# Gate differences at the head of the output products, casts that wait for one of them, and column tiles for two more key products

## The chip, the cores and the metric

The kernel runs on one core of one Trainium2 chip. The metric is device time in microseconds (us) of one execution. Each time below is the median of several executions, with the lowest and highest.

PE is TensorE's matmul stream, PEld its weight loads, DVE is VectorE, ACT ScalarE, POOL GpSimd, SP SyncE (which issues most of the DMAs here).

## The reference

Eight batches, eight heads, 576 tokens, head width 64. Queries are softmaxed over the head width, keys over the tokens; then two products give the attention output, which feeds a feed-forward block with a gate.

```python
kv  = einsum('bhsd,bhse->bhde', softmax(k, tokens), v)
x   = einsum('bhsd,bhde->bhse', softmax(q, width), kv)   # -> (4608, 512)
h   = x @ w_in                                           # (512, 2048)
g   = h * sigmoid(beta * h)
out = g @ w_out                                          # (2048, 512)
```

## The kernel before

The output product is done by a seven-product (Strassen-like) scheme: it needs sums of gate blocks (`g_sum1`, `g_sum2`) and two differences (`g_diff(0)`, the lower one, and `g_diff(1)`, the upper one; both write into the gates GT). A slab is 512 tokens; there are nine, and slabs 0 to 7 are batches 0 to 7 less 64 tokens each, which make up the last slab. `pass 1` is x @ w_in with the gates, `pass2_fast` the seven products. Into slab t's products the kernel mixes the attention work of batch t+1 by a list of (position, function), and calls hooks between products for that of batch t+2. In slabs 1 to 3 those hooks are written out one by one. Instructions of an engine run in the order in which they are added. The code below is abridged; comments stand for what is left out.

```python
def tiled(b):                 # key products as two column tiles of 64
    return b > 3

def attn_late(b):             # attention work of batch b in slab b-1
    ...
    if b < 4:
        s = spread(kv_steps(b, (0, 1)), 97, 101) + spread(kv_steps(b, (2, 3)), 101, 105)
        s += [(105, lambda: g_diff(1))]
        return s + spread(x[0:2], 117, 120)         # x: output steps (kv times QT)
    s = [(96, steps(kv_all, b)), (99, lambda: g_diff(1))]
    return s + spread(x, 107, 123)

def norm_turn(b, hp0):        # sums and 1/sums on DVE, scaling of EQ on POOL, DMA transpose to QT
    norm_main(b, hp0, 2, POOL)
    turn(b, hp0, 2)

def pass2_fast(t, tick, hooks):
    ...
    at(0)
    # product 1 (sums), product 2 (sums)
    # DVE: TS = product 1
    at(1)
    # DVE: TS -= product 2
    at(2)
    # product 3 (sums); DVE: TS -= product 3
    if t > 3:
        g_diff(0)
        g_diff(1)
    at(3)
    # product 4 (lower half, GT), product 5 (GT), product 6 (lower difference), product 7 (upper difference)

def casts(b):                 # POOL casts of the values: six where b is even, four where it is odd
    g = P.writer[("gs2", NG - 1)]                   # not before the last gate sum
    if b % 2 == 0:
        cast_vr(b, after=g)
    for hp in range(NHP):
        cast_v(b, hp, after=g)

if t == 1:
    on(0, exps, 2);  on(0, casts, 2)
    on(2, norm_turn, 2, 0);  on(3, norm_turn, 2, 2)
    on(3, g_diff, 0);  on(3, load, 4)
elif t == 2:
    on(0, exps, 3)
    on(2, norm_turn, 3, 0);  on(3, norm_turn, 3, 2)
    on(3, g_diff, 0);  on(3, load, 5)
    on(4, exp_q, 4);  on(4, casts, 4);  on(6, norm_turn, 4, 0)
```

The first two output steps of a batch below 4 come at positions 117 and 118.5 of the seven products, the last two in the first pass of the next slab, at 1 and 2.5:

```python
todo += [(1, steps(out_step, t, 2, MB, ACTE)), (2.5, steps(out_step, t, 3))]
```

The softmax here doesn't subtract the row's maximum and nothing guards it: scores larger than these inputs give would overflow.

Of the kernel before, what the change touches and what calls it, by code (L numbers as in the profile page):

```python
# [20 lines left out]
NG = NF // 2  # L21
# [134 lines left out]
def bass_efficient_attn_shen__then__act_swish_beta_kernel(  # L156
# [12 lines left out]
    with ExitStack() as es:  # L169
# [52 lines left out]
        P = Program()  # L222
# [156 lines left out]
        def bank(pool=MB):  # L379
            rot[0] += 1  # L380
            return pool[rot[0] % len(pool)]

        def mm(o, l, r_, start, stop, r=(), w=(), bk=0, tr=False):
            if tr:
                add(PE, lambda e: e.transpose(o, l, r_), r=r, w=w, bank=[bk])
            else:
                add(PE, lambda e: e.matmul(o, l, r_, start=start, stop=stop), r=r, w=w, bank=[bk])  # L387
# [22 lines left out]
        def kv_rows(b, hp, j):  # L410
            i = b % 2
            pi = (b // 2) % 2
            if j < 4:
                return (bass.AP(EK[i], hp * 512 + j * 128, [[2048, 128], [1, 128]]),
                        VB[i][:, j, hp, :], [("ek", i, hp)], [("vb", i, hp)], [("vone", i)])
            if b < 2:
                return (bass.AP(EKS[b], hp * 128, [[512, 128], [1, 128]]), VRS[b][:, hp, :],
                        [EKSK[b]], [("vrs", b)],
                        [("vrs0", b), ("vrsone", b, 0), ("vrsone", b, 1)])
            return (bass.AP(EKR[pi], hp * 128, [[512, 128], [1, 128]]),  # L420
                    VR[pi][b % 2][:, hp, :], [("ekr", pi, 0), ("ekr", pi, 1)],
                    [("vr", pi, b % 2)], [("vr0", pi, b % 2), ("vrone", pi, b % 2)])
# [2 lines left out]
            return b if b < 2 else 2 + b % 4  # L425

        def tiled(b):
            return b > 3

        def kvd(b, hp, bk, c):  # L430
            i = b % 2
# [7 lines left out]
        def kv_steps(b, hps, pool=MB):  # L439
            i = b % 2  # L440
            st = {}

            def one(n, hp, j):
                if n == 0 and j == 0:
                    st["b"] = bank(pool)
                bk = st["b"]
                l, r_, ke, kv, ko = kv_rows(b, hp, j)
                if not tiled(b):
                    mm(PS[bk][:, 256 * n:256 * n + VW - 1], l, r_[:, 0:VW - 1], j == 0, j == 4,
                       r=ke + kv, w=[("ps", bk)], bk=bk)  # L450
                for h in range(2) if tiled(b) else ():
                    p = slice(64 * h, 64 * h + 64)
                    add(PE, lambda e, h=h, p=p: e.matmul(  # L453
                        PS[bk][p, 256 * n:256 * n + D + 1], l[:, p], r_[:, HW * h:HW * h + D + 1],
                        start=j == 0, stop=j == 4, tile_position=(0, 64 * h),
                        skip_group_check=True),
                        r=ke + kv, w=[("ps", bk)], bank=[bk])
                if n == len(hps) - 1 and j == 4:
                    c, k_ = hps[0], len(hps)
                    s_ = bass.AP(PS[bk], D, [[512, 128], [256, k_]])  # L460
                    add(DVE, lambda e: e.reciprocal(RC[i][:, c:c + k_], s_),
                        r=[("ps", bk)], w=[("rc", i, h2) for h2 in hps], bank=[bk])
                    for m, h2 in enumerate(hps):
                        kvd(b, h2, bk, 256 * m)
            return [lambda n=n, hp=hp, j=j: one(n, hp, j) for n, hp in enumerate(hps)
                    for j in range(5)]
# [59 lines left out]
        def steps(fn, *a):  # L526
            return lambda: go(fn(*a))
# [12 lines left out]
        def attn_late(b):  # L540
            x = []
            for hp in range(NHP):
                x += out_step(b, hp, MB, ACTE if hp % 2 else DVE)
            if b < 4:
                s = spread(kv_steps(b, (0, 1)), 97, 101) + spread(kv_steps(b, (2, 3)), 101, 105)
                s += [(105, lambda: g_diff(1))]
                return s + spread(x[0:2], 117, 120)
            s = [(96, steps(kv_all, b)), (99, lambda: g_diff(1))]
            return s + spread(x, 107, 123)

        def spread(steps, lo, hi):
            return [(lo + (hi - lo) * k / len(steps), s) for k, s in enumerate(steps)]
# [8 lines left out]
        def go(steps):  # L561
            for s in steps:
                s()
# [154 lines left out]
        def g_diff(fh):  # L718
            f, th = NG * fh, 1 - fh
            add(DVE, lambda e: e.tensor_tensor(gv(f, th, NG), gv(f, th, NG), gv(f, 1 - th, NG),  # L720
                                               ALU.subtract),
                r=gk(f, 0, NG) + gk(f, 1, NG), w=gk(f, th, NG), war=True)
# [20 lines left out]
        def pass2_fast(t, tick, hooks):  # L743
            s, z5, z2 = HB[hrot[0] % 3], OB[0], OB[1]
            z2s = (OB[1], MB[0]) if t == NSLAB - 1 else (z2, z2)

            def prod(bk, lhs, lk, rhs, rk, first, end=False, part=range(NG)):
                two = bk == z2 and z2s[0] != z2s[1]
                for i, u in ([(i, u) for u in range(2) for i in part] if two and end else
                             [(i, u) for i in part for u in range(2)]):  # L750
                    l, r_ = lhs(i, u), rhs(i)
                    st = first and i == 0 and (u == 0 or two)
                    b_ = z2s[u] if two else bk
                    add(PE, lambda e, l=l, r_=r_, st=st, u=u, i=i, b_=b_: e.matmul(  # L754
                        PS[b_][:, 256 * u:256 * u + 256], l, r_, start=st, stop=end and i == NG - 1,
                        skip_group_check=True),
                        r=lk(i) + rk(i), w=[("ps", b_)], bank=[b_])
                    tick(32.0 / 56)

            def gt(f0, th):  # L760
                return (lambda i, u: GT[:, f0 + i, 256 * th + 128 * u:256 * th + 128 * u + 128],
                        lambda i: [("gt", f0 + i, th)])
# [5 lines left out]
            def wo(fh, dh):  # L768
                return (lambda i: WOUT[:, NG * fh + i, 256 * dh:256 * dh + 256],
                        lambda i: [("wout", NG * fh + i, dh)])  # L770
# [39 lines left out]
            def at(n):  # L810
                for f in hooks.get(n, ()):
                    f()

            at(0)
            def prod_s(part):
                prod(s, lambda i, u: GS1[:, i, 128 * u:128 * u + 128], lambda i: [("gs1", i)],
                     *wsum(0), True, True, part)
# [12 lines left out]
            for b_, u0, u1 in halves(z2):  # L830
# [1 line left out]
                add(DVE, lambda e, b_=b_, c=c: e.tensor_tensor(  # L832
                    TS[:, c], TS[:, c], PS[b_][:, c], ALU.subtract),
                    r=["ts", ("ps", b_)], w=["ts"], bank=[b_])
            if t > 3:
                g_diff(0)
                g_diff(1)
            at(3)
            prod(z5, *gt(0, 0), *wo(0, 1), False)
            copy(z5, 0, 1, ACTE)  # L840
            at(4)
# [21 lines left out]
        for t in range(NSLAB):  # L863
# [90 lines left out]
            def on(n, fn, *a):  # L954
                hooks.setdefault(n, []).append(lambda: fn(*a))
# [5 lines left out]
                    exp_kr(b)  # L961

            def casts(b):
                g = P.writer[("gs2", NG - 1)]
                if b % 2 == 0:
                    cast_vr(b, after=g)
                for hp in range(NHP):
                    cast_v(b, hp, after=g)

            if t == 1:  # L970
                on(0, exps, 2)
                on(0, casts, 2)
                on(2, norm_turn, 2, 0)
                on(3, norm_turn, 2, 2)
                on(3, g_diff, 0)
                on(3, load, 4)
            elif t == 2:
                on(0, exps, 3)
                on(2, norm_turn, 3, 0)
                on(3, norm_turn, 3, 2)  # L980
                on(3, g_diff, 0)
                on(3, load, 5)
                on(4, exp_q, 4)
                on(4, casts, 4)
                on(6, norm_turn, 4, 0)
            elif t == 3:
                on(0, exp_k, 4)
                on(0, exp_kr, 4)
                on(0, exp_q, 5)
                on(3, g_diff, 0)  # L990
                on(4, norm_turn, 5, 0)
                on(5, norm_turn, 5, 2)
                on(4, exp_qr)
                on(5, exp_k, 5)
                on(5, norm_turn_rem)
                on(5, casts, 5)
                on(5, load, 6)
                on(7, load_rem, "qrf", qt_h, QRF, 4)
            elif t + 2 < B:
                b = t + 2  # L1000
                on(0, exps, b)
                on(0, casts, b)
                if t == 4:
                    on(0, load, 7)
                on(3, norm_turn, b, 0)
                on(4, norm_turn, b, 2)
# [40 lines left out]
```

## Time and profile before

| | before |
|---|---|
| time, median of 3 | 273.59 us (273.55 to 273.74) |
| profiled span | 271.7 us, clock 1.0 |
| second pass of slab 1 begins | 60.65 us |
| second pass of slab 2 begins | 89.22 us |
| second pass of slab 3 begins | 117.57 us |
| last DVE instruction begins | 268.03 us |

The four marks in the lower rows divide the span into stages: 28.57 us ("slab 1": from its second pass to that of slab 2), 28.35 us ("slab 2", likewise), 150.46 us (the rest). The prediction shows the main lines of this profile. Two more views of it are needed later. First, from the page's table of costly groups: what it was, busy us and mean ns, then idle time of the engine before these instructions and what ended it.

```profile
L754 PE MATMUL PS<-WSUM,GT 128*128 128x256 bf16 x256 | 30.4, 273 | 0.5 <-DMA QT<-EQ 0.4
...
L720 DVE TENSOR_TENSOR GT<-GT 128x2048 bf16<-128x2048 bf16 x16 | 20.1, 1281 | 0.0
```

The products with a difference (PE) wait 0.5 us in the whole run, and 0.4 of it is one wait for the transposed queries. The 16 differences (DVE) take 1.28 us each on average. Second, POOL's timeline in slab 2 (start, length, what; instructions of one kind in a row are put together):

```profile
95.52 4.74 POOL L343 TENSOR_TENSOR EQ<-EQ,QI 128x1024 bf16<-128x1024 bf16 x2 [13.91 <-DVE QI L341]
100.39 2.16 POOL L372 CAST VR<-VRF 64x512 bf16<-64x512 f32 x2
```

The two casts of VR take 2.16 us here. The same two took 1.35 us in slab 1.

### The profile page before, as it was taken

The numbers are of one execution on the slowest core, as the hardware profiler recorded it, in microseconds if no ns is written. First come the engines' busy times: TensorE is split into PE (matmuls) and PEld (weight loads), VectorE is DVE, ScalarE is ACT, GpSimd is POOL, SyncE is SP. The second block draws the span as 40 slices with busy tenths as digits, with TensorE's granted clock in tenths as the row PEclk, the third lists the DMA queues.
The fourth block names the chain that finished last, engine by engine and source line by source line (L and its number), as shares of the span: only waits on it lengthen the run. The fifth ranks groups of instructions, "written<-read, shape, count | busy, mean of one in ns | idle before, by whom it ended". The sixth has DMA issues, their size and how long they took to land.

```text
span 271.7 us, 4811 instructions
## 1 busy us (share of the span) xinstructions
PE 263.8 (97%) x1882; PEld 165.7 (61%) x1905; DVE 194.0 (71%) x416; ACT 181.0 (67%) x284; POOL 64.1 (24%) x80
## 2 busy tenths in 40 slices
PE   8899999999999999999999999999999999999994
PEld 3444444448844885478646865687458745874683
DVE  4964586887867799878786977787687548626762
ACT  4898558789287956897778847893883387018610
POOL 2790010006530089000910870037000100000000
PEclk9999999999999999999999999999999999999999
DMA  7999999989799129930499999203800130012005
GB/s 220 314 201 207 227 321 349 303 227 373 173 337 285 65 53 299 332 95 2 89 282 283 308 345 182 103 20 65 208 0 2 31 142 2 0 69 88 0 5 152
DMA packets 59366, 45.93 MB, mean 169 GB/s; under 512 B 28608, under 2 KB 58320, under 8 KB 58320
## 3 DMA queue, kind: packets, MB, share of 16 engines
q1 hardware_dynamic: 54480, 40.90, 53.4%
q0 software_dynamic: 4240, 4.19, 9.4%
q10 hardware_dynamic: 624, 0.53, 0.6%
q8 instruction: 15, 0.25, 0.4%
q14 instruction: 7, 0.06, 0.1%
HBM read 36.71 MB, written 9.44 MB: 170 GB/s over the span
## 4 chain that ended last, share of the span: by engine, by line
PE 85%; DVE 4%; DMA 4%; POOL 2%; SPq 2%; issue 2%; ACT 1%; POOLq 0%
PE PS L387 51%; PE PS L754 33%; DMA VF<-in_v_dram 2%; DMA QT<-EQ 1%; PE PS L453 1%; POOL VB L358 1%; SPq L275 1%; DVE QS L339 1%; SPq L287 1%; DVE EQ L343 1%; POOL EQ L343 1%; DVE VB L358 1%; ACT GT L654 1%; POOL VR L372 0%; DVE QI L341 0%
## 5 line engine op out<-in xcount | busy, mean ns | idle before, releaser
L387 PE MATMUL PS<-XT,WIN 128*128 128x512 bf16 x562 | 126.2, 379 | 1.1 <-issue 0.3
L654 ACT ACTIVATE GT<-PS,BETA 128x512 bf16<-128x512 f32 x144 | 95.1, 689 | 37.8 <-PE PS L387 37.5
L387 PEld LDWEIGHTS PS<-XT,WIN 128*128 128x128 bf16 x576 | 55.2, 98 | 64.4 <-DVE XT L479 0.6
L677 DVE TENSOR_SCALAR GT<-GT,RB 128x512 bf16<-128x512 bf16 x144 | 52.1, 382 | 36.5 <-ACT GT L654 35.6
L343 POOL TENSOR_TENSOR EQ<-EQ,QI 128x1024 bf16<-128x1024 bf16 (+1 forms) x13 | 25.6, 1967 | 46.9 <-DVE QI L341 46.3
L754 PE MATMUL PS<-WOUT,GT 128*128 128x256 bf16 x256 | 33.0, 273 | 0.1
L754 PE MATMUL PS<-WOUT,GS 128*128 128x256 bf16 x256 | 31.9, 273 | 0.2
L754 PE MATMUL PS<-WSUM,GT 128*128 128x256 bf16 x256 | 30.4, 273 | 0.5 <-DMA QT<-EQ 0.4
L754 PEld LDWEIGHTS PS<-WSUM,GT 128*128 128x128 bf16 x256 | 25.0, 98 | 3.8 <-issue 0.3
L754 PEld LDWEIGHTS PS<-WOUT,GT 128*128 128x128 bf16 x256 | 24.9, 98 | 3.5
L790 ACT COPY O2S<-PS 128x512 f32<-128x512 f32 (+1 forms) x17 | 9.4, 560 | 25.6 <-PE PS L754 24.2
L754 PEld LDWEIGHTS PS<-WOUT,GS 128*128 128x128 bf16 x256 | 24.1, 98 | 3.4
L307 ACT ACTIVATE EQ<-QF 128x512 bf16<-128x512 f32 x32 | 17.9, 620 | 7.3 <-DMA QF<-in_q_dram 7.2
L358 POOL CAST VB<-VF 128x512 bf16<-128x512 f32 x24 | 16.7, 694 | 23.0 <-DVE GS L713 14.1
L713 DVE TENSOR_TENSOR GS<-GT 128x512 bf16<-128x512 bf16 (+2 forms) x32 | 21.9, 685 | 0.0
L339 DVE TENSOR_REDUCE QS<-EQ 128x16 f32<-128x1024 bf16 (+1 forms) x20 | 19.8, 991 | 0.9 <-ACT EQ L307 0.9
L720 DVE TENSOR_TENSOR GT<-GT 128x2048 bf16<-128x2048 bf16 x16 | 20.1, 1281 | 0.0
L307 ACT ACTIVATE EK<-KF 128x512 bf16<-128x512 f32 x32 | 18.1, 620 | 0.1
L479 ACT CAST XT<-PS 128x512 bf16<-128x512 f32 x18 | 10.3, 581 | 10.7 <-PE PS L387 10.7
L802 DVE TENSOR_TENSOR O2S<-TS,PS 128x512 f32<-128x512 f32 (+1 forms) x17 | 10.7, 643 | 9.5 <-PE PS L754 9.5
L754 PE MATMUL PS<-WSUM,GS 128*128 128x256 bf16 x128 | 16.7, 273 | 0.0
L387 PE MATMUL PS<-WOUT,GT 128*128 128x512 bf16 x62 | 15.0, 379 | 0.1
(82 smaller groups left out, 225.5 us busy)
## 6 DMA issues: line engine op xcount, KB each, us to landing
out_dram<-O2S SPq DMA_DIRECT2D x8, 1024.0 KB, 5.4
QF<-in_q_dram SPq DMA_DIRECT2D x6, 1024.0 KB, 5.9
KF<-in_k_dram SPq DMA_DIRECT2D x6, 1024.0 KB, 8.5
VF<-in_v_dram SPq DMA_DIRECT2D x6, 1024.0 KB, 12.2
KF<-in_k_dram SPq DMA_DIRECT2D x8, 256.0 KB, 5.5
VF<-in_v_dram SPq DMA_DIRECT2D x8, 256.0 KB, 5.5
WOUT<-in_moe_w_out_dram POOLq DMA_DIRECT2D x4, 512.0 KB, 16.4
WIN<-in_moe_w_in_dram POOLq DMA_DIRECT2D x3, 512.0 KB, 9.0
```

The lines of the kernel that those rows point to most:

```text
L307: add(ACTE, lambda e, o=o, a=a: e.activation(o, a, ACT.Exp), r=[(name + "f", i, hp)], w=[("e" + name, i, hp)])
L339: add(DVE, lambda e: e.tensor_reduce(s_, a, AX.X, ALU.add), r=ks, w=[("qs", i, hp0)])
L343: add(eng, lambda e: e.tensor_tensor(a, a, vb, ALU.mult), r=ks + [("qi", i, hp0)], w=ks)
L358: add(eng, lambda e: (e.copy if eng == ACTE else e.tensor_copy)(o, a), r=[("vf", i, hp), ("vone", i)], w=[("vb", i, hp)], after=after)
L387: add(PE, lambda e: e.matmul(o, l, r_, start=start, stop=stop), r=r, w=w, bank=[bk])
L479: add(eng, lambda e: (e.copy if eng == ACTE else e.tensor_copy)(XT[i][:, hp, :], PS[bk][:, :]), r=[("ps", bk)], w=[("xt", i, hp)], bank=[bk])
L654: add(ACTE, lambda e: e.activation(GT[:, f, :], PS[bk][:, :], ACT.Silu, scale=BETA[:, f:f + 1]), r=[("ps", bk), "beta"], w=[("gt", f, 0), ...
L677: add(DVE, lambda e: e.tensor_scalar(GT[:, f, :], GT[:, f, :], RB[:, f:f + 1], None, ALU.mult), r=k + ["rb"], w=k)
L713: add(DVE, lambda e: e.tensor_tensor(GS2[:, i:i + n, :], GT[:, i:i + n, :], GT[:, i + NG:i + NG + n, :], ALU.add), r=[k_ for f in (i, i + ...
L720: add(DVE, lambda e: e.tensor_tensor(gv(f, th, NG), gv(f, th, NG), gv(f, 1 - th, NG), ALU.subtract), r=gk(f, 0, NG) + gk(f, 1, NG), w=gk(f ...
L754: add(PE, lambda e, l=l, r_=r_, st=st, u=u, i=i, b_=b_: e.matmul(PS[b_][:, 256 * u:256 * u + 256], l, r_, start=st, stop=end and i == NG - ...
L802: add(DVE, lambda e, b_=b_, u0=u0, u1=u1: e.tensor_tensor(o[:, u0:u1, :], ts[:, u0:u1, :], bank3(b_)[:, u0:u1, :], ALU.add), r=["ts", ("ps ...
```

## The change

The intent, as far as the edit shows it: DVE stands idle before the first sum of the products, so one difference is put there; the other goes where the first sums are done. The differences and POOL's instructions get in each other's way (the prediction shows how), so the casts are made to wait for the upper difference. And the key products of batches 2 and 3 get the cheaper column tiles that batches 4 to 7 have.

```diff
         def tiled(b):
-            return b > 3
+            return b > 1
@@ attn_late
             if b < 4:
-                s = spread(kv_steps(b, (0, 1)), 97, 101) + spread(kv_steps(b, (2, 3)), 101, 105)
-                s += [(105, lambda: g_diff(1))]
+                s = [(101, steps(kv_all, b))]
                 return s + spread(x[0:2], 117, 120)
-            s = [(96, steps(kv_all, b)), (99, lambda: g_diff(1))]
+            s = [(96, steps(kv_all, b))]
@@ pass2_fast
+            g_diff(1)
             at(0)
@@ after the third sum
-            if t > 3:
+            if t > 2:
                 g_diff(0)
-                g_diff(1)
             at(3)
+            if t < 3:
+                g_diff(0)
@@ casts
-                g = P.writer[("gs2", NG - 1)]
+                g = P.writer[("gt", NG, 0)]
@@ hooks of slabs 1, 2 and 3, in each of them
-                on(3, g_diff, 0)
```

More of the change, by code (lines that the diff above doesn't have):

```diff
@@ L980, in bass_efficient_attn_shen__then__act_swish_beta_kernel @@
                 on(3, norm_turn, 3, 2)
-                on(3, g_diff, 0)
                 on(3, load, 5)
@@ L989, in bass_efficient_attn_shen__then__act_swish_beta_kernel @@
                 on(0, exp_q, 5)
-                on(3, g_diff, 0)
                 on(4, norm_turn, 5, 0)
```

## The prediction

> **What bounds the kernel now.** I started from the page's table of engines, then the chain of work that ended last, then the waits of PE and PEld by stretch, then the timelines of the stretches that the change edits.
>
> ```profile
> PE 263.8 (97%) x1882; PEld 165.7 (61%) x1905; DVE 194.0 (71%) x416; ACT 181.0 (67%) x284; POOL 64.1 (24%) x80
> PE 85%; DVE 4%; DMA 4%; POOL 2%; SPq 2%; issue 2%; ACT 1%; POOLq 0%
> ```
>
> The second line is the chain by engine. PE is the bound, at full granted clock, and after the first 50 us it almost never waits. So only two things are worth time: fewer PE cycles, or a change in one of the few PE waits that are left. The program runs nine slabs; each has a first pass (64 matmuls of 512 columns) and a second pass (112 matmuls of 256 columns, seven products). The second passes of slabs 1, 2 and 3 begin near 60.7, 89.4 and 117.6 us, and into those of slabs 1 and 2 the key products of batches 2 and 3 are mixed: these are what the change edits most.
>
> The PE waits left there are all for the transposed queries QT. In slab 1 the chain leaves PE altogether for ten microseconds:
>
> ```profile
> 62.25 0.34 DVE GS L713
> ...
> 62.72 0.61 POOL VR L372
> ...
> 66.22 0.61 POOL VB L358
> ...
> 66.96 1.91 POOL EQ L343
> ...
> 68.88 3.53 DMA QT<-EQ
> 72.41 0.27 issue
> 72.68 0.49 PE PS L754 x3
> ```
>
> Columns are start, length, what. The last sum of the gates (GS, done at 62.59) releases six POOL casts in a row, the scaling of EQ queues behind them on POOL, then comes the DMA transpose, and PE stands still until it lands at 72.41. Here POOL, not PE, sets the time. The timeline of DVE in the same stretch:
>
> ```profile
> 63.90 0.69 DVE L823 COPY TS<-PS 128x512 f32<-128x512 f32 x1 [1.32 <-PE PS L754]
> ...
> 68.51 0.25 DVE L341 RECIPROCAL QI<-QS 128x16 f32<-128x16 f32 x1
> 68.68 1.26 DVE L720 TENSOR_TENSOR GT<-GT 128x2048 bf16<-128x2048 bf16 x1
> ...
> 71.30 1.48 DVE L720 TENSOR_TENSOR GT<-GT 128x2048 bf16<-128x2048 bf16 x1
> ```
>
> The two L720 lines are the two gate differences; the bracket says that DVE sat idle 1.32 us before the first sum (L823). In slab 2 the same wait exists, smaller, and gated otherwise: there the casts came earlier, and EQ (95.52) follows the end of the first pass through exp, the reduction and the reciprocal. Weight loads of that stretch:
>
> ```profile
> 100.58 0.10 PEld L387 LDWEIGHTS PS<-QT,KVD 128*128 128x128 bf16 x1 [0.18 <-DMA QT<-EQ]
> ...
> 103.53 0.10 PEld L387 LDWEIGHTS PS<-QT,KVD 128*128 128x128 bf16 x1 [0.30 <-DMA QT<-EQ]
> ```
>
> PE reaches both output steps a little before the transpose lands.
>
> **What the Trainium skill says.** "SBUF — State Buffer", section "SBUF: two separate sides": DVE with two SBUF inputs and a GpSimd instruction lock a shared port pair for the whole instruction, whoever starts first, and the other blocks. The trace agrees: EQ on POOL takes 1.90 us in the median but 2.76 when it starts just after the 68.68 difference, and the difference at 71.30 takes 1.48 instead of 1.22 while that EQ still runs (to 71.70). "TensorEngine Tiling (Array Packing)", section "Theoretical Speedup", allows up to 2x for halves of 64 columns, and "Key Properties" says that a mode switch drains TensorE. The trace has both forms: tiled, 40 matmuls of 65 columns cost 0.75 us on the chain (19 ns each) with no gap around the block at 123.96; untiled, each of 20 matmuls of 131 columns costs 0.055 to 0.06, about 1.13 us. So tiling is worth 1.5x here and the drain isn't seen. "TensorE: Matmul & The Clock Gate", Part 1, puts the idle window that halves the clock at some 3.4 us; I expect no single stall that long, so no clock loss.
>
> **The change part by part.**
> (a) Column tiles for batches 2 and 3: 1.13 - 0.75 = 0.38 us of PE work less in slab 1 and in slab 2. They also start seven matmuls (0.76 us) later, at 67.6 in slab 1, just when EKR is ready (67.63), so the 0.22 us load wait for EKR goes. Sum if nothing else bound: about -0.9 us.
> (b) The upper gate difference opens the second pass. The last sum ends at 62.59; with a semaphore gap of 0.04 (as from L677 to L708 in the timeline) and 1.22 us of work it ends at 63.85, just ahead of the sum at 63.90. It fills the idle 1.32 us and delays nothing on DVE. The 1.2 us that it gives back later on DVE is off PE's path.
> (c) The lower difference stays after the second norm in slabs 1 and 2; in slabs 3 to 8 it keeps its place and just loses its neighbour. No PE product waited for either one before.
> (d) Casts wait for the upper difference instead of the last sum. Only slab 1 matters: the six casts move from 62.72 to 63.98 (+1.26). They take 4.24 us with what separates them (62.72 to 66.96), so EQ starts at 68.22 instead of 66.96. The reciprocal for it was done at 66.80, so POOL's queue is the gate and the 1.26 goes straight through. EQ (1.90) ends at 70.12. Transposes take 3.1 to 3.5 from issue to landing (median 3.3 in this stretch): 73.3 to 73.6 instead of 72.41, +0.9 to +1.2.
> Then a second effect. The lower difference is ready at 68.76 and now finds EQ running since 68.22. By the lock it starts at 70.12 and ends at 71.34; the second EQ goes after it, to 71.4 + 1.9 = 73.3, and its transpose lands at 73.3 + 3.1 = 76.4. PE asks for that half at 74.97 before; shifted by 0.9 to 1.2 it asks at 75.9 to 76.2 and waits to 76.4. So slab 1 hands over 76.4 - 74.97 = 1.45 us later.
> The product with the lower difference (first at 70.7 before, 70.1 now) stalls to 71.35 too, but its 13 matmuls end at 72.8, before the transpose at 73.3: hidden. The 0.6 us saved in slab 1 by (a) is hidden in the same way: PE arrives earlier and waits longer for a time that POOL sets.
> Slab 2: the sequence from first-pass end to both transposes isn't touched, so they land at the same offsets, and the 0.38 us of (a) turn into longer waits at the two lines shown above. Gain about 0.
> Slab 3: DVE is free 1.2 us earlier after its differences, so the casts of batch 5 (to 136.79) come earlier and a weight-load wait of 0.42 goes, of which PE shows only 0.10: -0.1.
> Slabs 4 to 8: no PE wait on what moves; 0.
> Sum: +1.45 + 0 - 0.1 = +1.35 us, 273.59 + 1.35 = 274.9.
>
> **The rivals.**
> 1. Tiling simply pays: -0.38 twice, -0.22 for EKR, -0.1 in slab 3, giving 272.5 to 272.9. For it: PE is 97% busy. Against it: it needs PE to have no wait just after the saving, and both slabs have one within 5 us, with a releaser that doesn't depend on PE's progress there. It would need the casts' delay to be absorbed, but POOL shows no gap from 62.72 to 71.70.
> 2. The lock goes the other way: the lower difference first, EQ blocked till about 69.98. Then the first transpose lands at 75 or so: +2 us, 275.5. Or POOL keeps the ports through both EQs, the lower difference ends near 73.3 and its product stalls PE: +2.3 us, 275.8. Against both: EQ starts half a microsecond before the difference is ready, and at 100.26 the waiting difference was served ahead of the next POOL cast (that cast, one of two, took 2.16 us together instead of 1.35).
> 3. The second half is hidden after all, and only the first landing counts: +0.9 - 0.1, 274.4. For it: the first transpose of slab 1 took 3.53 while loads were finishing, and may take 3.1 later.
>
> **Range and chances.** The step I trust most is the shift of POOL's queue by the length of one difference; what it does through the lock is less sure, and that spans 274.4 to 275.8. The gain of rival 1 would take a releaser that I have misread; I leave the lower edge open towards no change. Predicted 274.8 (a little under the sum, for the faster landing), 8 in 10 within 273.5 to 275.8. A change of 2% is 5.5 us, and none of the paths comes near: faster 0.01, same 0.98, slower 0.01.
>
> **What would show it.** In the changed kernel: the upper difference sits before the sum of the first product and takes about 1.22 us; VR's cast in slab 1 starts near 64.0, EQ near 68.2; the lower difference of slab 1 is stretched to about 2.5 us; PE's waits for QT grow from 0.4-0.5 to over 1 us in slab 1 and to about 0.5 in slab 2; the key blocks of batches 2 and 3 take 0.75 us. The prediction is wrong if PE's wait for QT in slab 1 shrinks, if POOL's EQ there starts before 67.5, or if the end of slab 2 moves by other than the end of slab 1.

## The result, and the profile after

| | before | after |
|---|---|---|
| time, median | 273.7 us (273.55 to 274.17, 6 runs) | 275.17 us (274.89 to 275.45, 6 runs) |
| profiled span | 271.7 us | 273.3 us |
| slab 1 to slab 2 | 28.57 us | 29.53 us |
| slab 2 to slab 3 | 28.35 us | 28.94 us |
| the rest | 150.46 us | 150.45 us |

The ratio is 1.005 (95% interval 1.0037 to 1.0063). Here and below a ratio is the mean time of one kernel's fast runs over that of the other's of the same rounds, so not quite the ratio of the medians that are quoted. The change costs about 1.5 us, half a per cent: the same by the measure of 2%, but clearly a loss. The stages say where: 0.96 us in slab 1, 0.59 us in slab 2, nothing after that. Another 0.10 us lies before slab 1, where nothing was edited; it is no part of the change.

From the page: the engines, the chain by engine, and the products with a difference.

```profile
PE 263.7 (96%) x1922; PEld 165.0 (60%) x1945; DVE 194.8 (71%) x416; ACT 181.0 (66%) x284; POOL 62.2 (23%) x80
...
PE 78%; DMA 8%; POOL 5%; DVE 4%; SPq 2%; issue 1%; ACT 1%; POOLq 0%; DVEq 0%
...
L753 PE MATMUL PS<-WSUM,GT 128*128 128x256 bf16 x256 | 30.4, 273 | 2.2 <-DMA QT<-EQ 1.3
```

PE does no more work than before, and the products with a difference wait 2.2 us in place of 0.5: the loss is waiting. PE's share of the chain falls from 85% to 78%, but not all of that is the change: from 8.4 to 18.9 us, where nothing was edited, the chain happens to run over POOL and a weight transfer this time, with 6.3 us less of PE. In slab 2, where it now leaves PE, it has 11.3 us less (90 to 106 us). The chain of waits in slab 1 (start, length, what):

```profile
62.35 0.35 DVE GS L712
...
62.72 1.24 DVE GT L719
...
64.08 0.62 POOL VR L372
...
67.59 0.62 POOL VB L358
...
68.29 1.91 POOL EQ L343
...
70.21 3.14 DMA QT<-EQ
73.35 0.27 issue
73.63 0.49 PE PS L753 x3
```

It is the chain of before with one link more: the difference (L719) stands between the last sum and the casts. EQ starts at 68.29 instead of 66.96, which is 1.33 us later (0.10 of it was there before). The transpose gives 0.39 back: it takes 3.14 us in place of 3.53. DVE in the same stretch:

```profile
62.72 1.23 DVE L719 TENSOR_TENSOR GT<-GT 128x2048 bf16<-128x2048 bf16 x1
64.01 0.69 DVE L824 COPY TS<-PS 128x512 f32<-128x512 f32 x1
...
68.78 2.48 DVE L719 TENSOR_TENSOR GT<-GT 128x2048 bf16<-128x2048 bf16 x1
```

The upper difference fits into the idle time before the first sum, which moves by no more than the head start of 0.10. The lower one, at 68.78, takes twice its time, because EQ has been running on POOL since 68.29. And PE there, with its waits in brackets:

```profile
71.41 1.58 PE L753 MATMUL PS<-WSUM,GT 128*128 128x256 bf16 x13 [0.90 <-DVE RC L461]
73.63 0.49 PE L753 MATMUL PS<-WSUM,GT 128*128 128x256 bf16 x3 [0.64 <-DMA QT<-EQ]
```

The first bracket names a reciprocal that came just after the difference on DVE; the product needs the stretched difference, which ended at 71.26. The second is the wait for the transpose.

Slab 2 has a chain that leaves PE now, where before it did not:

```profile
98.56 2.77 POOL EQ L343
101.33 0.02 issue
101.34 3.79 DMA QT<-EQ
105.13 0.05 issue
105.17 4.92 PE PS L387 x22
```

Here the second transpose takes 3.79 us. Before, the one at the same place, issued at 100.29, took 3.2; the trace's answer for the tile QT between 99.8 and 104 us:

```profile
DMA to landing us min/median/max: 3.2/3.2/3.2
```

EQ and the issue are as late as the whole slab, 1.06 us, so the 0.59 us are the transpose's own. POOL's timeline of the changed kernel and PE's weight loads beside it:

```profile
96.58 4.74 POOL L343 TENSOR_TENSOR EQ<-EQ,QI 128x1024 bf16<-128x1024 bf16 x2 [13.91 <-DVE QI L341]
101.45 1.34 POOL L372 CAST VR<-VRF 64x512 bf16<-64x512 f32 x2
```

```profile
101.87 0.10 PEld L387 LDWEIGHTS PS<-QT,KVD 128*128 128x128 bf16 x1 [0.70 <-DMA QT<-EQ]
...
105.17 0.10 PEld L387 LDWEIGHTS PS<-QT,KVD 128*128 128x128 bf16 x1 [0.79 <-DMA QT<-EQ]
```

The two VR casts now take 1.34 us: no difference holds them up any more, and they run from the moment at which the transpose is issued. The wait for that transpose, 0.30 before, is 0.79. What lies between the casts and the transpose is read from the DMA records, under e10.

### The profile page after: what moved, and what is told of

Same layout as the page of the kernel before. It is cut to its first block, busy times and chain, and to the rows that moved or that the text cites. A ratio compares the mean times of both kernels' runs of the same rounds, so it can differ in the third digit from the quotient of the medians.

```text
span 273.3 us, 4883 instructions
## 1 busy us (share of the span) xinstructions
PE 263.7 (96%) x1922; PEld 165.0 (60%) x1945; DVE 194.8 (71%) x416; ACT 181.0 (66%) x284; POOL 62.2 (23%) x80
## 4 chain that ended last, share of the span: by engine, by line
PE 78%; DMA 8%; POOL 5%; DVE 4%; SPq 2%; issue 1%; ACT 1%; POOLq 0%; DVEq 0%
PE PS L387 48%; PE PS L753 29%; DMA WIN<-in_moe_w_in_dram 3%; POOL EQ L343 3%; DMA QT<-EQ 3%; DMA VF<-in_v_dram 2%; PE PS L453 1%; POOL VB L358 1%; DVE QS L339 1%; SPq L275 1%; SPq L287 1%; POOL WIN L577 1%; ACT GT L653 1%; DVE EQ L343 0%; POOL VR L372 0%
## 5 line engine op out<-in xcount | busy, mean ns | idle before, releaser
L753 PE MATMUL PS<-WOUT,GT 128*128 128x256 bf16 x256 | 30.9, 273 | 0.1
L358 POOL CAST VB<-VF 128x512 bf16<-128x512 f32 x24 | 15.7, 652 | 25.5 <-DVE GT L719 16.9
L719 DVE TENSOR_TENSOR GT<-GT 128x2048 bf16<-128x2048 bf16 x16 | 20.8, 1302 | 0.3
```

Source lines behind the costliest of these rows:

```text
L358: add(eng, lambda e: (e.copy if eng == ACTE else e.tensor_copy)(o, a), r=[("vf", i, hp), ("vone", i)], w=[("vb", i, hp)], after=after)
L719: add(DVE, lambda e: e.tensor_tensor(gv(f, th, NG), gv(f, th, NG), gv(f, 1 - th, NG), ALU.subtract), r=gk(f, 0, NG) + gk(f, 1, NG), w=gk(f ...
L753: add(PE, lambda e, l=l, r_=r_, st=st, u=u, i=i, b_=b_: e.matmul(PS[b_][:, 256 * u:256 * u + 256], l, r_, start=st, stop=end and i == NG - ...
```

## The experiments

Theory A says that slab 1 pays for the position of the upper difference through POOL's queue (wait or port lock), that tiles alone gain nothing since PE runs into the next QT wait, and that slab 2 pays because the casts of batch 4 now run beside its second transpose. Rivals: the wait that was put into the casts is itself the cost (B); the tiles cost something (C); slab 2's loss is a late effect of slab 1 (D). The letters in the expectations are each run's own. Edits are against the changed kernel unless it says otherwise. Every run was correct. The table has the stage lengths of each profiled run; a stage that is not edited repeats to about 0.05 us where nothing but PE bounds it, and to 0.3 where a wait does: e11 and e12, and also e2 and e7, have the same code in slab 1 and differ by 0.31 and 0.26 there. The 0.96 us of slab 1 stand all the same: the changed kernel, e3, e6 and e10 give 29.53 to 29.57.

| run | time, us (lowest to highest) | ratio to before (95%) | slab 1 | slab 2 |
|---|---|---|---|---|
| before | 273.7 | 1 | 28.57 | 28.35 |
| changed | 275.17 (274.89 to 275.45) | 1.005 (1.0037, 1.0063) | 29.53 | 28.94 |
| e1 cast wait back | 275.01 (274.96 to 275.13) | 1.0054 (1.0042, 1.0066) | 29.28 | 28.96 |
| e2 tiles only | 273.59 (273.11 to 273.77) | 0.9998 (0.9986, 1.001) | 28.57 | 28.32 |
| e3 order only | 275.36 (275.17 to 275.73) | 1.0069 (1.0057, 1.0081) | 29.53 | 28.95 |
| e5 casts early | 275.02 (274.74 to 275.37) | 1.0053 (1.0041, 1.0065) | 29.35 | 28.96 |
| e6 slab 2 back | 274.75 (274.3 to 275.06) | 1.0034 (1.0021, 1.0046) | 29.57 | 28.33 |
| e7 slab 1 back | 274.68 (274.32 to 274.71) | 1.0028 (1.0014, 1.0042) | 28.83 | 28.97 |
| e8 tiles, later outputs | 274.75 (274.55 to 275.13) | 1.0041 (1.0028, 1.0053) | 28.70 | 29.25 |
| e9 changed, later outputs | 274.49 (274.4 to 274.66) | 1.0028 (1.0016, 1.0041) | 29.10 | 28.68 |
| e10 casts of batch 4 later | 274.78 (274.4 to 275.0) | 1.0038 (1.0025, 1.0052) | 29.54 | 28.31 |
| e11 combined | 273.35 (273.06 to 273.59) | 0.9993 (0.998, 1.0005) | 27.86 | 28.68 |
| e12 combined, one copy on ACT | 272.7 (272.33 to 273.0) | 0.9967 (0.9954, 0.9979) | 28.17 | 28.21 |

**e1: the casts of slab 1 wait for the last sum again.**

```diff
-                g = P.writer[("gt", NG, 0)]
+                g = P.writer[("gs2", NG - 1) if t == 1 else ("gt", NG, 0)]
```

> The changed kernel, with one wait undone: in slab 1 the casts of batch 2 wait for the last gate sum again, the upper difference stays in front. Theory A (the shared ports): the difference starts within 0.05 us of the last sum, the cast would start 0.13 us after it, finds the ports taken and is blocked to about the same moment as before, so EQ of slab 1 still starts near 68.2 to 68.4 and the time stays within 0.2 us of the changed kernel (275.0 to 275.3, some +1.3 us on the kernel before). Theory B (the wait itself is the cost): casts from 62.8, EQ from 67.0, the time falls back by about 1 us to 274.1. Theory C: cast and difference take turns, EQ starts near 67.6 and the time lies between.

275.01 us, and by its ratio nothing of the loss is gone; slab 1 is 0.25 shorter than in the changed kernel, which is within the scatter of stages. POOL's timeline of e1 in slab 1:

```profile
62.66 2.34 POOL L372 CAST VR<-VRF 64x512 bf16<-64x512 f32 x2 [22.43 <-DVE GS L712]
...
67.88 4.74 POOL L343 TENSOR_TENSOR EQ<-EQ,QI 128x1024 bf16<-128x1024 bf16 x2
```

The casts start at 62.66 as before, but the two of VR take 2.34 us instead of 1.35, since the difference on DVE started at 62.57 and holds the shared ports; EQ starts at 67.88, sooner than theory A expected (68.2 to 68.4) and later than its third theory (67.6). Counted from the start of its slab, EQ is 0.97 late against the kernel before, and 1.23 late in the changed kernel. So the lock alone does about four fifths of what the wait does, and the wait adds about 0.26 us. B falls as the main cause: it is the difference's position that costs.

**e2: the tiles alone, in the kernel before.**

```diff
-            return b > 3
+            return b > 1
-                s = spread(kv_steps(b, (0, 1)), 97, 101) + spread(kv_steps(b, (2, 3)), 101, 105)
+                s = [(101, steps(kv_all, b))]
                 s += [(105, lambda: g_diff(1))]
```

> The kernel before with only the column tiles for batches 2 and 3 (key block in one piece at the same place as in the changed kernel); gate differences and casts as before. Theory A (saving is hidden by the transposes): PE's waits for QT in slabs 1 and 2 grow by about 0.3 us each, the starts of the next first passes stay at 75.1 and 103.4, time within 0.2 us of before. Rival (PE-bound, tiles pay): 0.6 to 0.8 us faster than before. A second rival (the tiles themselves cost, by the mode switch): slower than before.

273.59 us, to the hundredth the median of before in that job, and the stages are the same to 0.03 us. The key block became cheaper (in slab 2 of the changed kernel it adds 0.85 us to the products around it; before, 1.14), and PE spends what it saved at the next wait. PE's timeline of e2 in slab 2:

```profile
100.83 0.49 PE L754 MATMUL PS<-WSUM,GT 128*128 128x256 bf16 x3 [0.44 <-DMA QT<-EQ]
```

The weight load of the same output step waited 0.49 us here, and 0.18 in the kernel before. C falls, and so does the hope in the tiles.

**e3: the order alone, without tiles for batches 2 and 3.**

```diff
-            return b > 1
+            return b > 3
```

> The changed kernel with the untiled key products for batches 2 and 3; order of the gate differences and waits of the casts as changed. Theory A: the loss is all in the order and the cast wait, so it is as slow as the changed kernel, within 0.2 us (+1.3 to +1.6 us on before), and PE's waits for QT are about 0.3 us shorter in slabs 1 and 2. Rival (tiles pay somewhere): a further 0.6 us slower than the changed kernel.

275.36 us, and both stages as in the changed kernel. With e2 this splits the change: the order does it, and the tiles do nothing that the stages show. (The ratio of e3 is 0.0019 above that of the changed kernel, with intervals that overlap; a few tenths of a microsecond from the tiles aren't excluded.)

**e5: the six casts of slab 1 go into its first pass, behind a gate scaling.**

```diff
+                    if t == 1 and n == 11:
+                        g = P.writer[("gt", ftile(n - 1), 0)]
+                        for hp in range(NHP):
+                            cast_v(2, hp, after=g)
+                        cast_vr(2, after=g)
-                on(0, casts, 2)
```

> The changed kernel with the six casts of batch 2 moved from the start of slab 1's second pass into its first pass (after the eleventh gate tile), where POOL is idle. Theory A (POOL's queue is the gate of the first transpose in slab 1): EQ of slab 1 now starts when its reciprocal is done, about 66.9 instead of 68.3, the first transpose lands near 72.4, and slab 1 gets its 1 us back: 274.1 or, if slab 2's longer transposes were chance, 273.7. It is not faster than before by more than 0.3, since the saving of the tiles stays hidden. Rival (the upper difference in front delays the queries' path in another way, through DVE): stays at 275. Side effect to watch: the casts may delay gate scalings near the end of the first pass.

275.02 us: no gain to speak of, where theory A had expected 274.1. POOL's and then PE's timeline of e5:

```profile
57.47 3.10 POOL L358 CAST VB<-VF 128x512 bf16<-128x512 f32 x4 [17.74 <-DVE GT L676]
...
67.69 4.74 POOL L343 TENSOR_TENSOR EQ<-EQ,QI 128x1024 bf16<-128x1024 bf16 x2 [5.29 <-DVE QI L341]
```

```profile
66.18 2.24 PE L753 MATMUL PS<-WOUT,GT 128*128 128x256 bf16 x17 [0.42 <-DVE TS L827]
```

The queue on POOL is gone (it sits idle 5.29 us before EQ), but the casts collide with the gate sums on DVE: the last sum ends near 63.5 instead of 62.7, everything behind it on DVE is late, a product on PE waits 0.42 us for a sum, and EQ is gated by DVE's reciprocal at 67.69. The cost went from one engine's queue to the other's.

**e6 and e7: the change taken back in slab 2 only (e6, T = 2), and in slab 1 only (e7, T = 1).** The upper difference returns to its late place there and the casts wait for the last sum.

```diff
-            g_diff(1)
+            if t != T:
+                g_diff(1)
@@ attn_late, b < 4
+                if b == T + 1:
+                    s += [(105, lambda: g_diff(1))]
@@ casts
-                g = P.writer[("gt", NG, 0)]
+                g = P.writer[("gs2", NG - 1) if t == T else ("gt", NG, 0)]
```

> The changed kernel with slab 2 alone put back: there the upper difference comes late again, between the key blocks and the output steps, and the casts wait for the last sum; slab 1 and the others as changed. In the changed kernel slab 1 hands over about 1.0 us later and slab 2 adds 0.6, since its second transpose lands 3.8 us after issue instead of 3.2. Theory A (that longer transpose comes from the order within slab 2): it is 3.2 again, the time is 274.5 to 274.7. Theory B (it comes from slab 1, whose delay moves the loads and the transposes against each other): it stays 3.8 and the time at 275.0 to 275.2.

> The changed kernel with slab 1 alone put back: upper difference late, casts of batch 2 behind the last sum as before; slab 2 and the others as changed. Theory A (order within slab 2 makes its second transpose longer): 3.8 us there and 274.0 to 274.3. Theory B (it comes from slab 1's delay): 3.2 there and the time of the kernel before, 273.5 to 273.8. In both, slab 1 ends where it ended before, with PE's wait for QT there at 0.9 us as in the kernel with tiles alone.

e6: 274.75 us; slab 1 29.57 as in the changed kernel, slab 2 28.33 as before, with a second transpose of 3.2 us. e7: 274.68 us; slab 2 28.97, with a second transpose of 3.8 us, though slab 1 is back at 28.83. So slab 2 pays on its own account whatever slab 1 does, and D falls. The two losses are separate and add up: 1.00 from e6's slab 1 and 0.62 from e7's slab 2.

e7 came out above what was expected of it (its slab 1 is 0.26 longer than before). PE's timeline of e7 in slab 1:

```profile
73.11 0.49 PE L755 MATMUL PS<-WSUM,GT 128*128 128x256 bf16 x3 [1.12 <-DVE GT L721]
```

The bracket names the late upper difference, but these three matmuls end the product with the lower one, and the weight load just before them waited for the transpose:

```profile
72.88 0.10 PEld L387 LDWEIGHTS PS<-QT,KVD 128*128 128x128 bf16 x1 [1.18 <-DMA QT<-EQ]
```

The difference merely ended last (72.94). That first transpose took 3.8 us here and 3.5 in e2, which has the same code in slab 1; this is the 0.26. It goes with earlier loads that are still moving data: between 69.4 and 69.9 us DMA moved 295 GB/s in e7, 164 in e2, and 33 in e11, where the transpose took 3.1. But the difference comes so close behind that it may be the next bound; the next pair of runs tests it.

**e8 and e9: the output steps later, so that PE comes to the transposed queries after they have landed;** e8 with the tiles alone (e2 and this), e9 with the whole change.

```diff
-                return s + spread(x[0:2], 117, 120)
+                return s + spread(x[0:2], 121, 124)
-                    todo += [(1, steps(out_step, t, 2, MB, ACTE)), (2.5, steps(out_step, t, 3))]
+                    todo += [(2.5, steps(out_step, t, 2, MB, ACTE)), (4, steps(out_step, t, 3))]
```

> A version meant to beat both: the kernel before with the column tiles alone, and the output steps of batches 2 and 3 about four matmul slots later (the first two nearer the end of the second pass, the last two 1.5 slots further into the next first pass), so that PE does other work while the transposes land. If the saving of the tiles is hidden by waits for QT, as I think, PE's waits for QT in slabs 1 and 2 fall from 1.5 us together (tiles alone) to under 0.5 and the time goes to 272.6 to 273.0. Rival: the output steps now come so late that the copies of XT hold up the next first pass, and nothing is gained (273.6).

> The changed kernel with the same later output steps. If its loss is waits for the transposes and nothing else, part of it comes back: the first wait in each slab goes (0.65 twice in PE), the second in slab 1 stays about 0.3, slab 2's second shrinks: 274.1 to 274.5. What stays over the version without the new order is then what the order costs beyond PE's slack: the stall of the product that waits for the lower difference, and the later second transposes. Rival: no change (275.1).

e8: 274.75 us, slower than before, and the expectation was wrong. PE's timeline of e8 in slab 1:

```profile
73.30 1.14 PE L754 MATMUL PS<-WSUM,GT 128*128 128x256 bf16 x7 [0.78 <-DVE GT L720]
```

PE no longer waits for the transpose, and waits 0.78 us for the late upper difference instead (the same in slab 2), and the late outputs come late for the next slab's first pass (its weight loads wait 0.41 and 0.56 us for copies on DVE). e9: 274.49 us, 0.7 below the changed kernel by the medians and 0.6 by the ratios, with the waits for the first transposes gone from PE's line. This is what "the difference first" may be good for: it takes away the bound behind the transpose. By itself it doesn't pay, because the transpose comes first. As a gain it isn't shown: e9 is 0.26 us below e8 by the medians, and the intervals of their ratios overlap.

**e10: only the casts of batch 4 in slab 2 moved,** two products later and behind an output sum.

```diff
-                g = P.writer[("gt", NG, 0)]
+                g = P.writer[("o2", t % 2, 2, 1) if t == 2 else ("gt", NG, 0)]
-                on(4, casts, 4)
+                on(6, casts, 4)
```

> The changed kernel; in slab 2 alone the six casts of batch 4 on POOL start later, after the third product is added up (some 2 us later than in the changed kernel, when the second transpose is through most of its way). The slab-by-slab runs showed that the order within slab 2 decides whether the second transpose there lands 3.2 or 3.8 us after issue; with the upper difference late, it held POOL's first cast back by about 1 us. Theory A (casts of POOL running beside the transpose lengthen it): 3.2 and 274.5 to 274.8. Theory B (not the casts): 3.8 and 275.0 to 275.3, and the cause stays open.

274.78 us, and slab 2 is back at 28.31. POOL's timeline of e10 in slab 2, then what the trace answers for the tile QT, of the changed kernel between 99.8 and 104 us and of e10 between 99.6 and 105 us:

```profile
103.92 1.35 POOL L372 CAST VR<-VRF 64x512 bf16<-64x512 f32 x2 [2.21 <-DVE O2S L801]
```

```profile
DMA to landing us min/median/max: 3.3/3.6/3.8
```

```profile
DMA to landing us min/median/max: 3.1/3.1/3.1
```

With POOL idle for 2.2 us after EQ, both transposes take 3.1 us; with the casts beside it, the second takes 3.8. Every trace fits this: 3.8 in the changed kernel, e1, e3, e5, e7 and e9, where the first cast starts within 0.2 us of the issue and takes its usual time; 3.1 to 3.2 before and in e2, e6 and e8, where it starts as early but the late difference holds it on the ports, so that two casts take 2.16 us, 0.8 more; 3.1 to 3.2 in e10, e11 and e12, where the casts start 1.3 us or more after the issue. In all of these, later casts run beside the rest of the transpose. The loads of batch 5 are issued 1.3 us after that transpose in the kernels before and after and in e10 alike, so they alone are not the difference.

So the time of the casts decides. It need not be the casts themselves, though: the DMA records show something else. These are the queues of the changed kernel from issue to landing of that transpose (101.34 to 105.13 us), then those of e10 (101.74 to 104.89), with packets, MB and share of the 16 DMA engines:

```profile
q1 hardware_dynamic: 1269, 0.48, 65.8%
q14 instruction: 1, 0.01, 0.5%
```

```profile
q1 hardware_dynamic: 1130, 0.34, 58.7%
```

One packet of 8 KB on a queue named "instruction" (by that name, a fetch of an engine's next instructions) falls into the changed kernel's transpose. Read packet by packet, the packed traces say the same of all: in the six runs with 3.8 us such a packet starts 2.58 to 2.61 us after the issue, just as the transpose's last packets go out; 15 of its 16 landing signals come within 3.2 us, as ever, and one at 3.8. In the seven runs with 3.1 to 3.2 no such packet lies between issue and landing (before, it starts at 103.97, after the landing at 103.49). In the six it starts 1.0 us after the first of the four casts that follow those of VR, so that holding or moving the casts seems to move it too. No run moved the packet without the casts, and the two last packets of the transpose are seen only 0.2 us late; how that makes 0.6 at the landing stays open.

**e11: all that helped, together.** The changed kernel with e9's later outputs and e10's later casts, two of slab 1's six casts in the first pass (e5 had all six), and the order of DVE and ACT for the output copies of batches 2 and 3 turned round.

```diff
+                    if t == 1 and n == 11:
+                        for hp in range(2):
+                            cast_v(2, hp, after=P.writer[("gt", ftile(n - 1), 0)])
-                x += out_step(b, hp, MB, ACTE if hp % 2 else DVE)
+                x += out_step(b, hp, MB, ACTE if (hp % 2 == 1) == (b > 3) else DVE)
```

> A second attempt to beat both: the changed kernel with the late output steps, two of the six casts of batch 2 moved into slab 1's first pass, well before its end, the casts of batch 4 late as in the run beside it, and the first output copy of batches 2 and 3 on ACT and the second on DVE. EQ of slab 1 should start near 67 (68.1 in the changed kernel with late outputs), so slab 1 is about 0.8 us shorter than there, and slab 2 about 0.5 if its second transpose is 3.2 again: 273.1 to 273.5, the kernel before or slightly better. Rival: the two early casts hold up the gate scalings so that EQ starts no earlier, as when all six were moved: 274.3.

273.35 us, level with before. POOL's timeline of e11 in slab 1, and PE's in slab 3's first pass:

```profile
66.99 4.74 POOL L343 TENSOR_TENSOR EQ<-EQ,QI 128x1024 bf16<-128x1024 bf16 x2 [0.26 <-DVE QI L341]
```

```profile
105.34 4.92 PE L387 MATMUL PS<-XT,WIN 128*128 128x512 bf16 x22 [0.62 <-DVE XT L479]
```

EQ is back at 66.99, now gated by the reciprocal and no longer by casts, and slab 1 is 0.7 us shorter than before. What is left is a copy on DVE that queues behind a reduction, 0.62 us.

**e12: that copy on ACT.**

```diff
-                    todo += [(2.5, steps(out_step, t, 2, MB, ACTE)), (4, steps(out_step, t, 3))]
+                    todo += [(2.5, steps(out_step, t, 2, MB, ACTE)), (4, steps(out_step, t, 3, MB, ACTE if t == 3 else DVE))]
```

> The combined version, with one copy moved: in slab 3's first pass the copy of the fourth output of batch 3 goes to ACT instead of DVE, where it queued behind a reduction (the wait of 0.62 us before 105.34 in the combined version). If that wait was worth its length: 0.4 to 0.6 us less than the combined version, 272.7 to 273.0 us, ratio 0.997 to 0.998 against the kernel before, and the wait gone from PE's line. If ACT is no sooner there (it scales gates at that place) or the third weight-load chunk has another wait behind it, nothing: 273.3 us, ratio 0.999. In neither case is 2% in sight.

272.7 us, ratio 0.9967 (0.9954 to 0.9979): the one version that beats both kernels, the one before by 0.8 us (273.52 in that job). PE's timeline at that place has no wait left:

```profile
103.83 4.37 PE L387 MATMUL PS<-XT,WIN 128*128 128x512 bf16 x18
```

## Why the prediction was right or wrong

The time (275.17 for 274.8) lay in the range, in its upper half, and "within 2%" held. By its own steps:

- **(a) Tiles gain nothing on the whole: right, shown by e2.** Two terms of it were off and cost nothing. The key block adds 0.85 us, so tiling saves 0.29 us and not 0.38. And "the drain isn't seen" was wrong, or at least there is a gap: about 0.1 us goes where PE enters the tiled block, 0.85 less the 0.75 that the tiled matmuls take (in the kernel before, too: 123.79 to 123.89). That the gap is the drain isn't shown. Two slips cost nothing: the terms of (a) add up to 0.98 and not to 0.9, and slab 2's second pass begins at 89.22, not 89.4.
- **(b) The upper difference is free on DVE: right.** It ran 62.72 to 63.95 and the sum behind it was not delayed.
- **(d) The casts carry the difference's length straight to EQ: right.** EQ at 68.29, predicted 68.22. e1 adds what the prediction did not separate: without the wait the lock costs some four fifths of it (EQ 0.97 late instead of 1.23, from the start of the slab).
- **(d), second effect, the lock on the lower difference: right in kind.** It took 2.48 us, predicted about 2.5. Rival 2, that the difference would win over EQ, didn't happen.
- **(d), the sum for slab 1: right mechanism, mis-sized.** "Slab 1 hands over 76.4 - 74.97 = 1.45 us later" measured 0.96. The second half's matmul came at 76.24, not after 76.4, because the second EQ ended at 73.03, not 73.3. And the subtraction set a landing against the time of a weight load: the matmul behind that load ran at 75.19 in the kernel before, 0.22 later, so that much was never lost. Nor was the second half the gate that the prediction made of it: 0.95 was lost at the first landing (PE's first matmul behind it at 73.63 for 72.68, 0.10 of it head start), and the second landing added 0.10.
- **"Slab 2: ... Gain about 0": wrong, and this is the step that failed.** It said that "the sequence from first-pass end to both transposes isn't touched". The sequence of releases was not; the length of one of its links was. The prediction itself quoted the 2.16 us of the held cast, as evidence on the lock, and did not ask what would move once that cast was no longer held. Measured: 0.59 us, the second transpose 3.8 for 3.2. e6, e7 and e10 show that it is slab 2's own and follows the casts' timing; the traces show a packet of the instruction queue inside the transpose in just the runs that have it.
- **"Slab 3: ... -0.1": wrong.** The rest of the run is 150.45 us for 150.46. Beyond the mark nothing was won.
- **Rival 1, tiling pays: didn't happen,** as e2 shows. **Rival 3, only the first landing counts, 274.4:** for slab 1 alone it was the nearest, since 0.9 was its term and 0.96 the result.

So it is luck that the total is close: two errors met, slab 1 put 0.49 too high and slab 2 0.59 too low. The sign that was named in advance for this, "if the end of slab 2 moves by other than the end of slab 1", did show. No clock was lost, as predicted: it stayed at 0.997 to 1.0.

What stays open: whether the instruction packet alone makes the transpose longer, since no run moved it without the casts; how much each of the five parts of e12 gives, as they were not each taken away again; and whether e12 needs the change at all, since no run has its moves in the kernel before.

## What to carry to other kernels

Before you move an instruction into an idle gap, look at who uses the same ports or waits for the same result in the other engines: the gap on DVE was real and free, and the loss came on POOL. Where a saving on the busiest engine is followed by a wait whose releaser doesn't depend on that engine, the saving is worth nothing until that wait is moved, so move the consumer (later outputs) together with it. And when a change takes away a hold-up, ask what the freed instruction will now run beside; if a transfer is slow for no visible reason, look at every DMA queue in its stretch, that of the instructions too. And a bracket that names what ended a wait names what came last: check it against what the instruction reads.

## What the Trainium skill lacked or had wrong

- "SBUF — State Buffer", section "SBUF: two separate sides": the lock of the shared ports is as it says. The difference took 2.48 us beside EQ and 1.23 alone, and two VR casts 2.34 us beside a difference and 1.35 alone.
- The same section says: "A DMA cannot be slowed by a compute op, and vice versa." A transpose of 3.8 us where POOL casts start beside it, and of 3.1 to 3.2 where they are held or moved, looks like an exception. The runs don't show one: in slab 2, in all six slow cases and in none of the seven others, a packet of the instruction queue lies inside the transpose.
- "Runtime: NRT & Kernel Launch", section "Instruction fetch mechanics", has nothing on a fetch that lies in another transfer's way. Here an 8 KB packet of the instruction queue, 2.6 us after the issue of a transpose, goes with 0.6 us until the last landing signal.
- "TensorEngine Tiling (Array Packing)", section "Key Properties", says that a mode switch drains TensorE, without a figure. Here PE loses about 0.1 us where it enters a tiled block of 40 matmuls (that this is the drain isn't shown), and the tiles save 0.29 us net of it.
- None of the pages read gives the time from issue to landing of a small DMA transpose from SBUF to SBUF. Here, 128 by 1024 of bf16: 3.1 to 3.2 us in most cases, and up to 3.9 with packets of other transfers in the way.
